# One DMA transpose for the keys of four heads in batches 2 and 3, in a talking-heads attention with a gated MLP behind it

## The chip, the core and the metric

The kernel runs on one core of one Trainium2 chip. The metric is the device time in microseconds, from the start of the program to its end on that core. Engines are named as in the profile: PE (matrix multiplications), DVE (vector), ACT (scalar), POOL (GpSimd), SP (the engine that issues all DMAs but three small ones at the start).

## The reference

Four batches, 12 heads, 448 positions, 64 numbers per head. The heads are mixed before and after the softmax, and the result goes through a gated MLP.

```
scores = (q @ k^T) / 8                            # per batch and head: 448 x 448
scores = einsum('bhij,hg->bgij', scores, w_pre)   # mix of heads
attn   = softmax(scores)
attn   = einsum('bhij,hg->bgij', attn, w_post)    # mix of heads
x      = attn @ v                                 # 448 x 768 per batch
u, v_  = split(gelu(x @ w_in))                    # 512 and 512 columns
gated  = u * (w_sg @ layernorm(v_) + b_sg)        # w_sg is 448 x 448
out    = x + gated @ w_out
```

## The kernel before, in words

Work goes by chunks of up to 128 query rows, four per batch, 16 in all; here they are called chunk 0 to chunk 15, so batch 1 is chunks 4 to 7, batch 2 is 8 to 11 and batch 3 is 12 to 15. A number is carried as a high and a low part in 16 bits, and a product of two such numbers is three matmuls.

`qk` (lines 961 to 1003) multiplies queries and keys of two heads (of four in the first, short chunk of a batch); the scores are scaled and copied out of PSUM, written to DRAM (`s_d`, line 958) and read back in groups of ten query rows over all heads (`g`, lines 1031 and 1037). Then come the first mix of heads (`ps_s`), the softmax (DVE maximum, ACT exponential, DVE reciprocal, a small scaling `wp` that is mostly on POOL), the second mix (`at`), the product with v (`ps_av`), and the MLP (`ps_v`, `ps_u`, `ps_x`). The MLP of one batch is done while the scores of the next are made: it is PE's filler around the change of batch.

Both operands of `qk` need the 64 numbers of a head along the partitions, so keys and queries are transposed. For batches 0 and 1 TensorE transposes the keys. For batches 2 and 3 (`B_DT = 2`) it is done by DMA, in `load_k`, in three loads per batch of four heads each (called K0, K1 and K2 here, for heads 0 to 3, 4 to 7 and 8 to 11). One load runs through these steps: SP fetches the 32-bit keys from DRAM (lines 548 and 550, three DMAs; for batches above 0 the last 64 positions are fetched twice, into partitions 0 to 63 and 64 to 127); two casts and two subtractions (lines 442 and 445, in the trace all on POOL) write the high and low parts into a staging tile of 16 bits, tag `sp`; SP transposes from the staging tile into `kT`. The queries of chunks 8 to 15 take the same way (`load_q`, line 489: one DMA transpose of twelve blocks of 128x128), through the same staging tile. **There is one buffer with the tag `sp`.** So K0, K1, K2 and the queries of each chunk use it one after the other: the next cast waits until the transposes before it have landed.

A load's transposes must also wait until the chunk of the batch before has used the keys that they overwrite: K0 of batch 2 waits for the `qk` of chunk 7 over heads 0 to 3, and so on.

The order of all instructions is fixed when the program is built, by a planner (`Plan`, line 252): it keeps a clock per engine, and picks among the streams of work by rank, plus a small random number (`jit`, seeded by `SEED`). A step on SP has a cost for the DMA engines and a number of issues (370 ns each on SP's clock): `(2500, 5)` for a load's transposes. Each engine then executes its instructions strictly in that order, and a semaphore holds an engine until what it needs is there. When the real times differ from the planned ones, an engine stands at an instruction that is not ready, with ready ones queued behind it.

Of the kernel before, what the change touches and what calls it, by code (L numbers as in the profile page):

```python
# [11 lines left out]
F16 = mybir.dt.float16  # L12
# [31 lines left out]
N_P32 = 3  # L44
N_PRE = 8
C_PRE = 800
SEED = 42
JIT = 0.2
SPIN = 110
SPIN_GAP = 200  # L50
# [57 lines left out]
def talking_heads_gmlp(ctx, tc, q, k, v, w_pre, w_post, w_in, g_ln, w_sg, b_sg, w_out, out):  # L108
    nc = tc.nc
    B, H, S, D = q.shape  # L110
# [3 lines left out]
    P = 128  # L114
# [3 lines left out]
    NC = S // TC  # L118
    JF = S // P
    JL = S - JF * P  # L120
    NA = JF * H + H // 2
    CQ = 120
    NCH = (S + CQ - 1) // CQ
# [13 lines left out]
    HG = 4  # L137
# [6 lines left out]
    ORD = (0, 1, 2, 3)  # L144
# [13 lines left out]
    const = ctx.enter_context(tc.tile_pool(name="const", bufs=1))  # L158
# [55 lines left out]
    mskc_t = vn_hi.rearrange("p c f -> p (c f)")[:, 504:520].bitcast(F32)  # L214


    kT = const.tile([P, H // HG, 2, HG // 2, S], F16, name="kT")
    qT2 = [const.tile([P, 2, H // 2, P], F16, name=f"qT{i}") for i in range(2)]
    v32 = const.tile([P, NA, D], F32, name="v32")
    at32 = const.tile([P, NA, AW], F32, name="at32")  # L220
# [39 lines left out]
    class Plan:  # L260
# [8 lines left out]
        def __init__(self):  # L269
# [7 lines left out]
            self.size = {}  # L277
            self.rnd = random.Random(SEED)

# [6 lines left out]
        def free(self, *names):  # L286
            return self.after([self.res.get(n, 0) for n in names])

        def seen(self, *names):
            return self.after([self.tm.get(n) for n in names])  # L290
# [4 lines left out]
        @staticmethod  # L295
        def after(times):
            return None if None in times else max(times)
# [6 lines left out]
        def give(self, t, *names):  # L304
            for n in names:
                assert self.res[n] is None, n
                self.res[n] = t
# [95 lines left out]
    def ones(n):  # L403

        return {"act": 100 + 0.9 * n, "dve": Shared(70 + 0.52 * n), "pool": 75 + 1.06 * n}
# [28 lines left out]
    free, seen, past, after, take, give, chain = pl.free, pl.seen, pl.past, pl.after, pl.take, pl.give, pl.chain  # L434


    def cast(o, i, scale=1.0, e=None):
        e = e or pl.on
        if e is nc.scalar:
            e.activation(out=o, in_=i, func=AF.Copy, scale=scale)  # L440
        else:
            e.tensor_scalar(out=o, in0=i, scalar1=scale, scalar2=1.0, op0=ALU.mult, op1=ALU.mult)  # L442

    def diff(o, a, b, e=None):
        (e or pl.on).tensor_tensor(out=o, in0=a, in1=b, op=ALU.subtract)  # L445
# [8 lines left out]
    def turn(ps, src, width):  # L454

        for n, x in enumerate(src):
            rows = x.shape[0]
            tr(ps[:, n * width:n * width + rows], x, ident32[:rows, :rows])
# [6 lines left out]

    def turn_k(hg, t, a, ps):
        turn(ps, [t[:, a, cc] for cc in range(JF)] + [t[:JL, a, JF]], P)
        return (ps[:, :S], *(kT[:, hg, k, a, :] for k in range(2)))

    def load_q(i):  # L470
        rank = K_Q12[i - 1] if i < 3 else fin[i - 1] - K_Q
# [49 lines left out]
    def load_kv():  # L521
        todo = [(b * GPB + (0, 3, 6)[hg] + (3 if b else 0), "v", b, hg) for b in range(B) for hg in range(H // HG)]
        for b in range(1, B):
            i = NCH * b - 1
            for hg in range(H // HG):
                todo.append((fin[i] + hg * HG * (fin[i + 1] - fin[i]) // H - K_KV, "k", b, hg))
        todo.sort()
        for rank, kind, b, hg in todo:
            if kind == "v":
                if ("v", b, hg) not in tm:  # L530
                    t = yield "sp", 2000, rank, 0, lambda: seen(("av", b - 1, ORD[-1])) if b else 0
                    fetch_v(b, hg, t)
                continue
            t = yield "sp", 2000, rank, 0, lambda: free(ring("st"), ring("sp"))
            load_k(b, hg, rank + 1, t)

    def fetch_v(b, hg, t):
        hs = slice(hg * HG, (hg + 1) * HG)
        nc.sync.dma_start(out=v32[:, hg * HG * JF:(hg + 1) * HG * JF].rearrange("p (h c) d -> p h c d", c=JF),
                          in_=v[b, hs, :JF * P].rearrange("h (p c) d -> p h c d", c=JF))  # L540
        if hg == H // HG - 1:
            for f in range(2):
                nc.sync.dma_start(out=v32[f * JL:(f + 1) * JL, JF * H:], in_=v[b, f * H // 2:(f + 1) * H // 2, JF * P:].rearrange("h p d -> p h d"))
        tm["v", b, hg] = t

    def fetch_k(b, h0, x):
        hs = slice(h0, h0 + HG)
        nc.sync.dma_start(out=x[:, :, :JF], in_=k[b, hs, :JF * P].rearrange("h (p c) d -> p h c d", c=JF))
        for f in range(2 if b else 1):
            nc.sync.dma_start(out=x[f * JL:(f + 1) * JL, :, JF], in_=k[b, hs, JF * P:].rearrange("h p d -> p h d"))  # L550
# [9 lines left out]
    def load_k(b, hg, rank, t0):  # L560
        h0 = hg * HG
        x, xname = staged("st")
        y, name = staged("sp")
        k32 = y.rearrange("p t a c b d -> p (t a c b d)").bitcast(F32).rearrange("p (a c e) -> p a c e", a=2, c=NC)
        fetch_k(b, h0, x)

        def turns_by_dma(t):
            for part in range(2):
                t = yield None, (ones, twos)[part](HG * NC * D), rank, t
                for a in range(2):  # L570
                    o = y[:, part, :, :, a, :]
                    if part:
                        diff(o, x[:, a::2], y[:, 0, :, :, a, :])
                    else:
                        cast(o, x[:, a::2])
            give(t, xname)
            t = yield "sp", (2500, 5), rank, t, lambda: seen(("qk", NCH * b - 1, h0 + HG - 1))
            for w in range(2):
                for a in range(HG // 2):
                    nc.sync.dma_start_transpose(out=kT[:, hg, w, a, :JF * P].rearrange("p (c j) -> p c j", c=JF),  # L580
                                                in_=y[:, w, a, :JF].rearrange("p c b d -> p (c b d)"))
                    nc.sync.dma_start_transpose(out=kT[:, hg, w, a, JF * P:], in_=y[:JL, w, a, JF].rearrange("p b d -> p (b d)"))  # L582
            give(t, name)
            tm["k", b, hg] = t

        def turns(t):
            t = yield None, ones(HG * NC * D), rank, t
            for a in range(2):
                side(pl.on, k32, x, a)
            give(t, xname)  # L590
            ends = []
            for a in range(2):
                t1 = yield "pe", 4 * C_TR, rank, t, lambda: after([work_free(), seen(("qk", NCH * b - 1, h0 + HG - 1))])
                ps, bank_name = work_bank("ps_k")
                split(rank, t1, turn_k(hg, k32, a, ps), S, bank_name, ends)
            give(t1, name)
            yield None, {"pool": 0}, rank, t1, lambda: max(ends) if len(ends) == 2 else None
            tm["k", b, hg] = max(ends)

        pl.add((turns_by_dma if b >= B_DT else turns)(t0))  # L600
# [6 lines left out]
    def ring(kind):  # L607
        return f"{kind}{stn[kind] % {'st': 2, 'sp': 1}[kind]}"

    def staged(kind):  # L610

        name = ring(kind)
        stn[kind] += 1
        take(name)
        if kind == "st":
            return st32.tile([P, HG, NC, D], F32, tag="st", name="st32"), name
        return st16.tile([P, 2, HG // 2, NC, 2, D], F16, tag="sp", name="st16"), name
# [196 lines left out]
    def work_free():  # L814
        return free(f"wk{works[0] % 2}")
# [47 lines left out]
    def part_mm(s, hg, ps):  # L863
        for n, (tq, tk) in enumerate(((0, 0), (0, 1), (1, 0))):
            for o in range(2):
                for a in range(2):
                    r = slice(a * D, (a + 1) * D)
                    m = QP * (2 * o + a)
                    mm(ps[m:m + QP, :S], lhsT=qT2[0][r, tq, 2 * hg + o, PART[s]:PART[s] + QP],
                                     rhs=kT[r, hg, tk, o, :], start=(n == 0), stop=(n == 2))  # L870

    def part_hi(s, hg, ps, eng=None):
        cast(e0[s][:, hg, 0], ps[:, :S], 1.0 / math.sqrt(D), eng)
# [45 lines left out]
    def qk_mm(i, h, pss):  # L919

        rows = q_rows(i)
        for n, (tq, tk) in enumerate(((0, 0), (0, 1), (1, 0))):
            for o in range(heads(i) // 2):
                w = 64 if quarters(i) else rows
                for c in range(0, rows, w):
                    m = min(w, rows - c)
                    for a, ps in enumerate(pss):
                        r = slice(a * D, (a + 1) * D)
                        mm(ps[o * rows + c:o * rows + c + m, :S], lhsT=qT2[i % 2][r, tq, h // 2 + o, c:c + m],
                                         rhs=kT[r, h // HG, tk, h // 2 % 2 + o, :], start=(n == 0), stop=(n == 2))  # L930

    def qk_place(i, h):
        if (i, h) in early:
# [106 lines left out]
    st = {}  # L1040
# [556 lines left out]
    with tc.manual_schedule():  # L1597
# [13 lines left out]
        for i, w in enumerate((w_pre, w_post)):  # L1611
# [4 lines left out]
                              in_=ident32[:H, :H].unsqueeze(1).unsqueeze(1).to_broadcast([H, 2, NH, H]))  # L1616
# [201 lines left out]
```

## Time and profile before

| | |
|---|---|
| median of three runs | 612.03 us (611.52 to 621.69) |
| the profiled execution | 613.37 us, of which the traced span is 611.6 us |
| PE busy | 573.4 us (94%) |
| ACT, DVE, POOL busy | 372.0, 362.2, 221.7 us (61%, 59%, 36%) |
| PE's share of the chain that ended last | 79%; DMA 6%, SP's queue 4% |
| instructions in the trace | 25,636 |

The chain that ended last is followed back from the last instruction to what released each step; where it is on PE, PE had work and did it, and where it is on a DMA or on SP's queue, PE was waiting for that. A window is a stretch of the span, in us from its start; the granted clock (PEclk) is 1.00 at 2.4 GHz and 0.50 at 1.2 GHz, and between them where a stretch has both.

### The profile page before, as it was taken

To read this page: it belongs to the slowest core of one execution; us is meant where nothing else is said; L and a number is where in the kernel's file an instruction comes from. 1 tells how busy PE (TensorE), PEld (TensorE's weight loads), DVE (VectorE), ACT (ScalarE), POOL (GpSimd) and SP (SyncE) were. 2 spreads that over 40 slices of the span, in tenths; PEclk is the share of its full clock that TensorE was granted. 3 is DMA by queue.
4 is the path that set the end of the run, shared out by engine and by line. 5 is a ranking of instruction groups with operands and counts; after the bars stand their busy time and mean duration, and the time that the engine had idled before them with its cause. 6 is when DMAs were issued, how large, how long until landed. Compare 5 with 4: busy or idle time off the path is not lost.

```text
span 611.6 us, 25636 instructions
## 1 busy us (share of the span) xinstructions
PE 573.4 (94%) x10847; PEld 382.3 (62%) x10847; DVE 362.2 (59%) x945; ACT 372.0 (61%) x911; POOL 221.7 (36%) x392
## 2 busy tenths in 40 slices
PE   8997999999999979489999989789999999999997
PEld 4555766577665637257766756446765857678654
DVE  6865487666667533246777655336768764355560
ACT  5776697786867535346877555446766665655231
POOL 6424255774455363223413463123312252121100
PEclk9998999999999999889999997879999999999999
DMA  9887999986888396399898775399796745420002
GB/s 201 240 250 219 246 303 263 212 246 201 243 270 252 101 223 162 84 226 267 203 250 244 171 203 165 93 247 248 145 273 181 202 125 171 121 73 4 1 2 91
DMA packets 110611, 113.48 MB, mean 186 GB/s; under 512 B 60852, under 2 KB 97724, under 8 KB 110496
## 3 DMA queue, kind: packets, MB, share of 16 engines
q1 hardware_dynamic: 110432, 111.84, 68.2%
q8 instruction: 85, 1.39, 1.0%
q14 instruction: 30, 0.25, 0.2%
q10 hardware_dynamic: 64, 0.00, 0.0%
HBM read 64.20 MB, written 42.10 MB: 174 GB/s over the span
## 4 chain that ended last, share of the span: by engine, by line
PE 79%; DMA 6%; SPq 4%; issue 3%; POOL 2%; ACT 2%; DVE 2%; POOLq 0%; ACTq 0%; DVEq 0%
PE at L236 15%; PE ps_s L236 12%; PE ps_x L236 12%; PE ps_av L236 10%; PE ps_v L236 9%; PE ps_qk L236 9%; PE ps_u L236 9%; DMA qT<-st 2%; DMA g<-s_d 1%; DMA s_d<-s 1%; SPq L580 1%; SPq L582 1%; PE ps_q L240 1%; POOL st L445 1%; DMA v<-in_v_dram 1%
## 5 line engine op out<-in xcount | busy, mean ns | idle before, releaser
L1077 DVE TENSOR_REDUCE nm<-ps_s 128x1 f32<-128x448 f32 x180 | 105.6, 618 | 47.6 <-PE ps_s L236 46.4
L1084 ACT ACTIVATE p<-ps_s,nm 128x448 f32<-128x448 f32 x180 | 113.7, 632 | 30.1 <-DVE nm L1077 29.5
L236 PEld LDWEIGHTS at<-wp,p 64*64 64x64 f32 x5364 | 108.8, 139 | 32.2 <-issue 19.8
L440 ACT ACTIVATE at<-at 128x420 f32<-128x420 f32 x179 | 99.2, 567 | 45.6 <-PE at L236 44.8
L236 PE MATMUL at<-wp,p 64*64 64x60 f32 (+1 forms) x5364 | 114.8, 223 | 6.8 <-issue 4.1
L442 POOL TENSOR_SCALAR wp<-wpc,rs 128x60 f32<-128x60 f32 x139 | 46.5, 336 | 193.5 <-DVE rs L1090 146.8
L440 ACT ACTIVATE s<-ps_qk 128x448 f16<-128x448 f32 (+3 forms) x134 | 68.4, 546 | 35.6 <-PE ps_qk L236 26.5
L236 PE MATMUL ps_qk<-kT,qT 64*64 64x448 f16 (+3 forms) x1080 | 72.8, 360 | 16.5 <-DMA qT<-st 11.2
L236 PE MATMUL ps_av<-at,v 128*64 128x120 f32 (+3 forms) x1536 | 71.2, 261 | 1.4 <-issue 1.4
L236 PEld LDWEIGHTS ps_av<-at,v 128*64 128x64 f32 (+1 forms) x1536 | 65.0, 135 | 9.5 <-issue 6.5
L949 DVE SCALAR_TENSOR_TENSOR s<-ps_qk,s 128x448 f16<-128x448 f32 x84 | 49.8, 618 | 26.5 <-ACT s L440 25.7
L236 PE MATMUL ps_u<-xTh,wbuf 128*128 128x256 f16 (+1 forms) x384 | 61.3, 260 | 0.0
L236 PE MATMUL ps_x<-wo,gbuf 128*128 128x384 f16 (+1 forms) x336 | 58.5, 339 | 0.0
L1089 DVE TENSOR_SCALAR rs<-ss 128x1 f32<-128x1 f32 x180 | 26.9, 149 | 52.3 <-ACT p L1084 50.5
L236 PEld LDWEIGHTS <-wbuf 128*128 128x128 f16 x576 | 50.2, 98 | 11.1 <-issue 6.6
L236 PEld LDWEIGHTS <-qT 64*64 64x64 f16 (+3 forms) x1080 | 30.1, 106 | 42.8 <-issue 13.2
L236 PE MATMUL ps_s<-g,wpre 60*64 60x448 f32 x324 | 46.9, 571 | 4.1 <-ACT p L1084 4.0
L236 PE MATMUL ps_u<-xTl,wbuf 128*128 128x192 f16 (+1 forms) x192 | 49.8, 259 | 0.0
L236 PEld LDWEIGHTS <-gbuf 128*128 128x128 f16 (+1 forms) x384 | 31.0, 103 | 23.5 <-issue 8.0
L1313 DVE SCALAR_TENSOR_TENSOR xTl<-ps_av,xTh 128x360 f16<-128x360 f32 (+1 forms) x32 | 15.3, 501 | 41.8 <-ACT xTh L440 41.8
L236 PEld LDWEIGHTS <-xTh 128*128 128x128 f16 (+1 forms) x336 | 24.5, 102 | 22.5 <-issue 11.3
L440 ACT ACTIVATE xTh<-ps_av 128x360 f16<-128x360 f32 (+1 forms) x31 | 12.4, 450 | 41.3 <-PE ps_av L236 41.3
(215 smaller groups left out, 903.1 us busy)
## 6 DMA issues: line engine op xcount, KB each, us to landing
g<-s_d SPq DMA_DIRECT2D x166, 210.0 KB
s_d<-s SPq DMA_DIRECT2D x18, 448.0 KB
s_d<-s SPq DMA_DIRECT2D x24, 280.0 KB
v<-in_v_dram SPq DMA_DIRECT2D x12, 384.0 KB
out_dram<-ot SPq DMA_DIRECT2D x24, 192.0 KB
s_d<-s SPq DMA_DIRECT2D x18, 252.0 KB
s_d<-s SPq DMA_DIRECT2D x18, 224.0 KB
s_d<-s SPq DMA_DIRECT2D x18, 196.0 KB
```

The source lines that it names most:

```text
L236: nc.tensor.matmul(ps, lhsT=lhsT, rhs=rhs, **kw)
L240: nc.tensor.transpose(*args)
L440: e.activation(out=o, in_=i, func=AF.Copy, scale=scale)
L442: e.tensor_scalar(out=o, in0=i, scalar1=scale, scalar2=1.0, op0=ALU.mult, op1=ALU.mult)
L445: (e or pl.on).tensor_tensor(out=o, in0=a, in1=b, op=ALU.subtract)
L580: nc.sync.dma_start_transpose(out=kT[:, hg, w, a, :JF * P].rearrange("p (c j) -> p c j", c=JF), in_=y[:, w, a, :JF].rearrange("p c b d -> ...
L582: nc.sync.dma_start_transpose(out=kT[:, hg, w, a, JF * P:], in_=y[:JL, w, a, JF].rearrange("p b d -> p (b d)"))
L949: nc.vector.scalar_tensor_tensor(out=e[:, 1, :], in0=ps[:n, :S], scalar=1.0 / math.sqrt(D), in1=e[:, 0, :], op0=ALU.mult, op1=ALU.subtract)
L1077: nc.vector.tensor_reduce(out=nm, in_=st[n]["s2"][:, :S], axis=AX.X, op=ALU.max, negate=True)
L1084: nc.scalar.activation(out=x["p32"], in_=x["s2"][:, :S], func=AF.Exp, bias=x["nm"], accum_out=x["ss"])
L1089: nc.vector.tensor_scalar(out=x["rs"], in0=x["ss"], scalar1=1e-9, scalar2=1.0 / S_P, op0=ALU.add, op1=ALU.mult)
L1313: nc.vector.scalar_tensor_tensor(out=dl, in0=src, scalar=isc, in1=dh, op0=ALU.mult, op1=ALU.subtract)
```

## The change

The eight DMA transposes of a load (for each part and each pair of heads one of three blocks of 128x128, and one that takes 64 partitions to 64 columns) become one of sixteen blocks of 128x128. To make that possible a row of `kT` gets 512 columns in place of 448: the last block is transposed whole, with the second copy of the 64 positions in columns 448 to 511, which nobody reads. The places that read `kT` take the first 448 columns. The planner's figures change with it: `(2800, 5)` for the transposes, `(2200, 3)` for the fetch of keys, `(2400, 3)` for the last fetch of v, and another seed.

```diff
-SEED = 42
+SEED = 21
...
-    kT = const.tile([P, H // HG, 2, HG // 2, S], F16, name="kT")
+    kT = const.tile([P, H // HG, 2, HG // 2, NC * P], F16, name="kT")
...
-        return (ps[:, :S], *(kT[:, hg, k, a, :] for k in range(2)))
+        return (ps[:, :S], *(kT[:, hg, k, a, :S] for k in range(2)))
...
-                    t = yield "sp", 2000, rank, 0, lambda: seen(("av", b - 1, ORD[-1])) if b else 0
+                    t = yield "sp", (2400, 3) if hg == H // HG - 1 else 2000, rank, 0, lambda: seen(("av", b - 1, ORD[-1])) if b else 0
...
-            t = yield "sp", 2000, rank, 0, lambda: free(ring("st"), ring("sp"))
+            t = yield "sp", (2200, 3), rank, 0, lambda: free(ring("st"), ring("sp"))
...
-            t = yield "sp", (2500, 5), rank, t, lambda: seen(("qk", NCH * b - 1, h0 + HG - 1))
-            for w in range(2):
-                for a in range(HG // 2):
-                    nc.sync.dma_start_transpose(out=kT[:, hg, w, a, :JF * P].rearrange("p (c j) -> p c j", c=JF),
-                                                in_=y[:, w, a, :JF].rearrange("p c b d -> p (c b d)"))
-                    nc.sync.dma_start_transpose(out=kT[:, hg, w, a, JF * P:], in_=y[:JL, w, a, JF].rearrange("p b d -> p (b d)"))
+            t = yield "sp", (2800, 5), rank, t, lambda: seen(("qk", NCH * b - 1, h0 + HG - 1))
+            nc.sync.dma_start_transpose(out=kT[:, hg].rearrange("p t a (c j) -> p (t a c) j", c=NC),
+                                        in_=y.rearrange("p t a c b d -> p (t a c b d)"))
...
-                                     rhs=kT[r, hg, tk, o, :], start=(n == 0), stop=(n == 2))
+                                     rhs=kT[r, hg, tk, o, :S], start=(n == 0), stop=(n == 2))
...
-                                         rhs=kT[r, h // HG, tk, h // 2 % 2 + o, :], start=(n == 0), stop=(n == 2))
+                                         rhs=kT[r, h // HG, tk, h // 2 % 2 + o, :S], start=(n == 0), stop=(n == 2))
```

Since the planner's figures and its seed change, the order of the whole program changes, on every engine. The amount of work does not: PE has the same matmuls but for two used to pass the time, and only a few copies go to another engine. Three places around the change of batch matter below.

SP, from the fetch of K2 of batch 2 to the transpose of the first queries of that batch (chunk 8, into `qT_124`), before. `st_4346` holds fetched keys, `st_4347` is the staging tile, `st_4642` the same buffer with queries:

```order
L548 DMA st_4346<-in_k_dram 128x4x192
L550 DMA st_4346<-in_k_dram 64x4x64 x2
L1563 DMA out_dram<-ot 64x384 x2
L1037 DMA g_120<-s_d_136 60x2x448 x2
L1563 DMA out_dram<-ot 128x384
L580 DMA_TRANSPOSE kT<-st_4347 128x3x128
L582 DMA_TRANSPOSE kT<-st_4347 128x64
...
L1563 DMA out_dram<-ot 128x384
L1037 DMA g_119<-s_d_136 60x2x448 x2
L489 DMA_TRANSPOSE qT_124<-st_4642 128x12x64
```

The same queue of the changed kernel, from the transpose of K0 of batch 2 to the fetch of K1 (`st_4134`); the writes to `s_d_136` are scores of chunk 7:

```order
L578 DMA_TRANSPOSE kT<-st_3689 128x16x128
L955 DMA s_d_136<-s_3857 128x896
L955 DMA s_d_136<-s_3893 128x896
L1034 DMA g_119<-s_d_136 60x2x448 x2
L1034 DMA g_120<-s_d_136 60x2x448 x2
L489 DMA_TRANSPOSE qT_124<-st_4005 128x12x64
L955 DMA s_d_136<-s_4064 128x896
L452 DMA q_91<-in_q_dram 56x12x64
L452 DMA q_91<-in_q_dram 72x12x64
L548 DMA st_4134<-in_k_dram 128x4x192
L550 DMA st_4134<-in_k_dram 64x4x64 x2
```

The queries of chunk 8 came after K2; now they come after K0, ahead of K1 and K2. Those of chunk 9 now stand between K1 and K2.

POOL, from the cast of K2 of batch 2 to the queries of chunk 8, before:

```order
L442 TENSOR_SCALAR st_4347<-st_4346 128x8x64 x2
L442 TENSOR_SCALAR wp<-wpc_101,rs 128x60
L445 TENSOR_TENSOR st_4347<-st_4346,st_4347 128x8x64 x2
L442 TENSOR_SCALAR wp<-wpc_101,rs 128x60 x2
L442 TENSOR_SCALAR st_4642<-q_91 64x768
L445 TENSOR_TENSOR st_4642<-q_91,st_4642 64x768
L442 TENSOR_SCALAR wp<-wpc_101,rs 128x60 x4
```

POOL in the changed kernel, from the cast of K0 of batch 2 (`st_3689`) through the queries of chunk 8 (`st_4005`); `vs` and `gbuf` are the gate of batch 1's MLP:

```order
L442 TENSOR_SCALAR st_3689<-st_3688 128x8x64 x2
L442 TENSOR_SCALAR wp<-wpc_101,rs 128x60
L445 TENSOR_TENSOR st_3689<-st_3688,st_3689 128x8x64 x2
L442 TENSOR_SCALAR wp<-wpc_101,rs 128x60 x3
L442 TENSOR_SCALAR st_4005<-q_91 64x768
L1504 TENSOR_TENSOR vs<-vs,gbuf 128x448
L445 TENSOR_TENSOR st_4005<-q_91,st_4005 64x768
L1504 TENSOR_TENSOR vs<-vs,gbuf 128x448
L445 TENSOR_TENSOR gbuf<-vs,gbuf 128x448 x2
```

The cast of queries now stands behind K0 and ahead of most of the gate, where it was behind K2 and behind the whole gate.

PE, just ahead of the first `qk` of chunk 8 (it reads `qT_124`), before; the last `qk` of chunk 7 is 295 rows further up, and between the two stand 128 matmuls of `ps_x`, 24 of `ps_s`, 192 of `at` and 48 of `ps_av`:

```order
L236 MATMUL ps_x<-wo,gbuf 128x384
L236 LDWEIGHTS xTh_129
L236 MATMUL ps_x<-ident_x,xTh_129 128x128
L236 LDWEIGHTS xTl_130
L236 MATMUL ps_x<-ident_x,xTl_130 128x128
...
L236 LDWEIGHTS qT_124
L236 MATMUL ps_qk<-kT,qT_124 64x448
```

The same place in the changed kernel, from the last matmul of chunk 7's `qk` (it reads `qT_125`):

```order
L236 MATMUL ps_qk<-kT,qT_125 64x448
L236 MATMUL ps_s_4302<-g_119,wpre_98 64x448 x2
L236 MATMUL ps_s_4303<-g_119,wpre_98 64x448 x2
L236 MATMUL at_472<-wp,p_112 64x60 x12
L236 MATMUL at_472<-wp,p_108 64x60 x12
L236 MATMUL at_472<-wp,p_112 64x30 x4
L236 MATMUL at_472<-wp,p_108 64x30 x4
L236 LDWEIGHTS qT_124
L236 MATMUL ps_qk<-kT,qT_124 64x448
```

The first `qk` of chunk 8 has moved ahead of most of batch 1's MLP: it stands directly behind chunk 7, and the rest of that MLP now lies between the `qk` of chunk 8 that need K0, K1 and K2: 30 matmuls of `ps_x` ahead of the one for K1, 90 more ahead of the one for K2.

## Rows read from the trace of the kernel before

**Rows 1.** The page's first part: busy us, share of the span, instructions.
```profile
PE 573.4 (94%) x10847; PEld 382.3 (62%) x10847; DVE 362.2 (59%) x945; ACT 372.0 (61%) x911; POOL 221.7 (36%) x392
```

**Rows 2.** Windows by stage: stretch, its length, busy us of each engine, PEclk, DMA share, GB/s.
```profile
197.00:276.00 79.00, 65.21 (x1304) 40.79 (x1301) 31.79 (x91) 36.47 (x93) 28.28 (x45) 0.91 0.66 159
276.00:340.00 64.00, 63.43 (x1402) 44.48 (x1398) 47.54 (x130) 47.38 (x119) 24.63 (x45) 1.00 0.92 242
340.00:410.00 70.00, 59.89 (x1175) 39.21 (x1177) 33.40 (x87) 33.11 (x83) 24.56 (x35) 0.88 0.65 168
```

**Rows 3.** Waits of PE from 197 to 276 us: us in total, times, longest.
```profile
PE ps_qk L236 <- DMA qT<-st: 9.7, 1, 9.7
PE ps_s L236 <- ACT p L1084: 4.0, 2, 2.7
```

**Rows 4.** Waits of PE from 340 to 410 us.
```profile
PE ps_qk L236 <- DMA kT<-st: 4.9, 3, 2.2
PE ps_s L236 <- ACT p L1084: 3.1, 2, 2.6
PE ps_qk L236 <- DMA qT<-st: 1.5, 1, 1.5
```

**Rows 5.** Timeline of SP's queue, K2 of batch 2: start, us, what.
```profile
233.24 0.41 SPq L548 DMA_DIRECT2D st<-in_k_dram  x1
...
241.72 1.23 SPq L580 DMA_TRANSPOSE kT<-st  x1
```

**Rows 6.** Timeline of POOL there, with its idle time before and what ended it.
```profile
240.49 1.20 POOL L442 TENSOR_SCALAR st<-st 128x512 f16<-128x512 f32 x2 [4.19 <-DMA g<-s_d]
...
241.94 2.28 POOL L445 TENSOR_TENSOR st<-st,st 128x512 f16<-128x512 f32 x2
...
255.58 0.82 POOL L442 TENSOR_SCALAR st<-q 64x768 f16<-64x768 f32 x1 [10.77 <-DMA g<-s_d]
```

**Rows 7.** The chain that ended last, 195 to 262 us: start, us, what.
```profile
196.88 0.91 PE ps_s L236 x8
197.79 4.62 PE ps_av L236 x96
...
204.22 1.06 PE at L236 x64
205.28 0.57 PE ps_qk L236 x12
...
252.88 2.39 DMA kT<-st
...
258.14 3.31 DMA qT<-st
```

**Rows 8.** The same chain, 340 to 412 us.
```profile
348.27 2.94 PE ps_x L236 x15
...
385.93 2.39 PE ps_x L236 x18
...
400.98 6.72 DMA qT<-st
```

**Rows 9.** Instructions of kT and of qT: ns shortest/median/longest, first and last start.
```profile
L582 SPq DMA_TRANSPOSE kT<-st x24: 1202/1227/2506, 200.9 to 395.7; - x24
...
L489 SPq DMA_TRANSPOSE qT<-st x8: 1252/1654/3193, 258.1 to 439.3; - x8
```

**Rows 10.** Windows in which PE's clock was low while it worked, columns as above.
```profile
227.00:232.00 5.00, 5.00 (x85) 2.89 (x82) 1.89 (x6) 1.96 (x6) 1.27 (x3) 0.66 0.23 46
262.00:266.00 4.00, 4.00 (x87) 2.29 (x83) 1.69 (x3) 1.48 (x4) 1.78 (x2) 0.67 0.97 265
...
368.30:374.00 5.70, 5.70 (x98) 3.94 (x97) 3.03 (x11) 2.99 (x8) 1.83 (x3) 0.51 0.22 43
...
398.10:406.00 7.90, 7.51 (x100) 4.44 (x100) 2.63 (x6) 2.86 (x7) 3.39 (x6) 0.59 1.04 255
```

**Rows 11.** The window over K2's transposes, columns as above.
```profile
242.00:252.00 10.00, 9.78 (x192) 6.04 (x190) 4.54 (x17) 7.25 (x20) 2.81 (x4) 1.00 0.19 39
```

## The prediction

> **What bounds the kernel now.** I read the page first. PE is busy 573.4 of 611.6 us and no other engine passes 61% [rows 1], so the kernel is PE's work plus the time in which PE stands or runs slowly, and the second part is all that this change can touch: 38.2 us stand idle. Then I cut the span by stage to see where. The two stretches around a change of batch, 197 to 276 and 340 to 410 us, have PE busy 65.2 of 79.0 and 59.9 of 70.0 us [rows 2]: 13.8 and 10.1 us idle, 23.9 of the 38.2. The stretch between them loses 0.6 of 64. So outside the two changes of batch PE loses 14.3 us in 462.6, some 3%.
>
> The idle time costs more than itself. The granted clock in these stretches is 0.91 and 0.88 on the mean [rows 2], and after each wait PE works at 1.2 GHz for some microseconds [rows 10]. Work lost is length times one minus the clock: 5.0 x 0.34 = 1.7, 4.0 x 0.33 = 1.3, 5.7 x 0.49 = 2.8, 7.9 x 0.41 = 3.2, together 9.0 us. So the two changes of batch cost 23.9 + 9.0 = 32.9 us above PE's work at full clock.
>
> The waits of PE say for what. At the first change it is one wait of 9.7 us for the queries' transpose, and 4.0 us for ACT's exponential [rows 3]; at the second 4.9 us for the keys' transposes, 1.5 us for the queries' and 3.1 us for the exponential [rows 4]. What stands behind the 9.7 us is told by SP, POOL and the chain of waits: K2's fetch is issued at 233.24, POOL casts from 240.49 and subtracts to 244.2, SP issues eight transposes from 241.72 [rows 5, 6], the last at 252.88, and that lands 2.39 us later, at 255.27 [rows 7]; only then is the staging tile free, POOL casts chunk 8's queries at 255.58 (it stood 10.77 us, with four `wp` queued behind) [rows 6], and their transpose goes out at 258.14 and lands after 3.31 us [rows 7]. PE starts again at 261.5. So one tile, held from cast to landing, is what is late, and 13.6 us of each hold (241.72 to 255.27) are transposes.
>
> **What the change removes.** An issue of one block of 64 columns takes 1.2 us of SP [rows 9], one of three blocks 1.23 [rows 5], one of twelve 1.25 to 3.19, median 1.65 [rows 9]. So an issue is priced by the piece, hardly by its blocks: eight take at least 9.6 us, one takes 1.3 to 3.2. That issues and not the transfer fill the 13.6 us shows in the DMA share, 0.19 while K2's transposes run [rows 11].
>
> The new transpose is not in the trace. The nearest rows are the queries' of twelve blocks, issue to landing 3.31 and 6.72 us [rows 7, 8], the second with the DMA engines full (share 1.04) [rows 10]. Scaled by 16/12: 4.4 and 9.0 us. Since waits that vanish bring the traffic closer to that of 276 to 340 us (share 0.92) [rows 2], I take 8, nearer the loaded row, and 6 for the queries'. Each load's transposes then shrink from 13.6 to 8, by 5.6 us (4.6 to 9.2 at the ends). One loss goes against it: before, the first transposes went out while POOL still subtracted (241.72 against 244.2) [rows 5, 6]; one transpose of the whole tile must wait for both, 2.5 us. So the net is 3.1 us for each load, 2.1 to 6.7 at the ends, three loads at each change of batch. The 14% more blocks (16 for 14) are in the 8; the longer rows of `kT` cost PE nothing, since it reads 448 columns as before.
>
> The Trainium skill (Advanced Engine Details and Errata, X-Bar Transpose (TRN2)) says that transpose DMAs on TRN2 run as fast as others, 350 to 400 GB/s. An estimate from that page: sixteen blocks of 32 KB, 524 KB, in 1.5 us at 350. The trace doesn't bear it out: twelve blocks, 393 KB, in 3.31 us are 119 GB/s [rows 7]. By the page's rate the new waits in the sum below would go, and it would come to 585.
>
> **What the new order asks for.** I count from t, the end of chunk 7's (then chunk 11's) `qk` over heads 2 and 3, for which K0's transpose waits. Prices of PE's work are from the chain: 64 `at` records (32 in the order) 1.06, 96 `ps_av` (48 in the order) 4.62, 8 `ps_s` (4 in the order) 0.91, 12 `qk` 0.57 [rows 7], `ps_x` and the like 0.13 each, and 0.20 in the gate [rows 8].
>
> First change. From t to chunk 8's first `qk` PE has 160 `at` (5.3), 16 `ps_s` (3.6), 72 `ps_x` (48 of the gate, some of them half-height pairs; 11), 9 `ps_u` (1.2) and four `qk` (2.3): t+23. To the `qk` that needs K1 it is 12 more, t+36; to that for K2 some 20 more, t+56. The loads: K0's transpose goes out at t+2, behind a score write, and lands at t+10. POOL casts and subtracts chunk 8's queries, with a product of the gate between, in 5.5 us; their transpose goes out at t+15.5 and lands at t+21.5, before PE asks. K1's fetch stands two issues behind it, t+17.5; fetch to cast takes 7.3 us (233.24 to 240.49), cast and subtraction 3.7 [rows 5, 6]: out at t+28.5, landed at t+36.5, 0.5 late. Then chunk 9's queries take the tile (2.5 us), K2's fetch follows their transpose at t+41, cast from t+48.5, out at t+52, landed at t+60: 3.5 late.
>
> Second change. Chunk 12's queries were transposed long before. PE has some 38 us from t to the `qk` for K0 and 44 to that for K2. K2's fetch is held on SP by the scores of heads 8 and 9, to t+25.5: cast t+33, out t+36.5, landed t+44.5, 0.5 late.
>
> So 4.5 us of new waits remain, at the half clock seen after each [rows 10] some 6. Before, PE did batch 1's whole MLP by 251.8 and then stood; now it is spread between the three loads. The exponential's waits (4.0 and 3.1) hang on POOL: `wp` stood behind casts that waited for late keys [rows 6]. They go with the lateness; a cast that waits for one landing remains, in front of the gate.
>
> **The sum**, against the profiled execution, 613.4 us (1.3 above the median of three, 612.0): minus 32.9 for the two changes of batch, plus 3% of their 149 us, 4.6, as everywhere else, plus 6 of new waits: 591.1. I say **591**.
>
> At nothing I cost the new order elsewhere. It is covered by the engines' slack alone (POOL 36%, DVE 59%, ACT 61% busy) [rows 1]; a new draw can win or lose part of the 14.3 us that PE stands idle outside the two stretches, say 5 either way. SP's time saved (some 8 us per load, of a queue that also issues scores and `g`) I cost at nothing too: it only moves transfers earlier.
>
> **Rivals.**
> - *The loaded end and POOL's new place.* At 9 us per transpose and 6.7 for the queries' the same count gives 8.7 us of waits, some 11 with the clock: 596. What could add to it is POOL: the cast of chunk 8's queries now stands in front of nine products of the gate. If K0's transpose is held up on SP by a score write, the gate slips by as much, and with it the output products meant to fill PE: 8 to 10 us back, 600 to 606. For it: full stretches have a DMA share of 0.92 to 1.04 [rows 2, 10], and POOL did stand 10.77 us at such a cast [rows 6]. Against: the means at the changes of batch are 0.66 and 0.65 [rows 2].
> - *The transfer is what takes the time* (slower). If the 13.6 us were transfer and not issue, sixteen blocks would take 15.5. In the new order, with chunk 9's queries between K1 and K2 and no overlap with the subtraction, the count gives: chunk 8's first `qk` 3 us late, K1 12, K2 11, and K2 of the second change 12: 38 us where 23.9 stood, at like clock about 627. It decides from some 12 us per transpose, where the waits equal the old ones. Against it stand the share of 0.19 [rows 11] and twelve blocks in 3.31 to 6.72 [rows 7, 8]. The Trainium skill (DMA: Bandwidth & Descriptors, Issuing engines are not separate DMA queues) speaks for it: the sequencer's time to start a DMA is usually small relative to the DMA itself. By that rule fewer issues save next to nothing; here the trace contradicts it, with 9.6 us of issues in 13.6.
> - *The new draw loses elsewhere* what it wins here: 10 us more on PE's 14.3 give 601, 20 give 611.
>
> **How the numbers follow.** The forecast, 580 to 599, gets 0.66; POOL's place 0.13; the new draw 0.14, nearly all of it within 2%; the transfer 0.07. Two per cent, about what a measurement of this kernel can tell from no change, is 599.8 and 624.3. Faster 0.66, within 0.26, slower 0.08 (the transfer, and 0.01 of the draw). The lower end is the sum without new waits, 585, and 5 us won by the draw: 580. The upper end takes in POOL's place and most of the draw: 611. Outside remain the transfer and a little on each side.
>
> **What would show it.** In the profile of the changed kernel: six issues at line 578, of 1.3 to 3.2 us, in place of 48; each lands in 4.4 to 9 us (15 or more: the transfer). PE's wait of 9.7 us for `qT<-st` gone, waits for `kT<-st` below 5 us each; idle time in the two changes of batch together at most 12 us, and the granted clock there above 0.95. POOL's waits in front of the queries' casts 5 to 7 us in place of 10.77. If these hold and the time is above 600, the draw took it, and the stretch that lost it shows in the windows. The forecast is wrong if a transpose takes over 10 us, or if PE finds a new wait at the moved `qk`.

## The result, and the profile after

The changed kernel takes 578.06 us (median of four, 576.36 to 580.17), the kernel before 616.86 (median of four, 611.52 to 627.43). The ratio is 0.9451, with a 95% interval from 0.9389 to 0.9512; it leaves out the executions of a slower state, here two of the kernel before (621.69 and 627.43), and so goes by its other two, 611.52 and 612.03. The change is faster, by more than was forecast: 591 stood in the prediction, and 578 lies just below its lower end, 580. The profiled execution took 576.36 us, 37.0 less than the one of before (613.37).

The page of the changed kernel: its span, the engines' busy time (as [rows 1] of before), the granted clock in 40 slices, and the chain that ended last.

```profile
span 574.6 us, 25573 instructions
...
PE 560.2 (97%) x10845; PEld 377.2 (66%) x10845; DVE 362.6 (63%) x942; ACT 376.5 (66%) x925; POOL 218.0 (38%) x381
...
PEclk9999999999999998999999999999999999999999
...
PE 89%; DMA 4%; ACT 2%; issue 2%; DVE 2%; POOL 1%; SPq 0%; ACTq 0%; POOLq 0%
```

PE does the same work in 560.2 us in place of 573.4, and stands idle for 14.4 in place of 38.2. So 23.8 of the 37.0 us are idle time, and 13.2 are busy time, most of it work that was done at a low clock before (see the sizes below).

The changed kernel's windows around the two changes of batch and between them, as [rows 2] show them of before (length, busy us of each engine, PEclk, DMA share, GB/s):

```profile
190.00:262.00 72.00, 68.74 (x1412) 42.90 (x1406) 37.29 (x102) 43.08 (x110) 32.54 (x46) 0.98 0.96 215
262.00:325.00 63.00, 62.80 (x1399) 45.12 (x1391) 46.66 (x125) 46.48 (x116) 22.58 (x41) 1.00 0.91 233
325.00:385.00 60.00, 58.08 (x1298) 38.49 (x1296) 36.84 (x97) 37.87 (x96) 26.25 (x40) 1.00 0.94 231
```

PE is idle for 3.3 and 1.9 us where it was idle for 13.8 and 10.1, the clock is 0.98 and 1.00 for 0.91 and 0.88, and the DMA engines, idle for a third of the time before, are as full there as between. What PE still waits for, at the first change (190 to 265 us) and then at the second (325 to 385), against [rows 3, 4]:

```profile
PE at L236 <- issue: 2.8, 2, 1.9
PE ps_s L236 <- issue: 0.3, 1, 0.3
```
```profile
PE ps_qk L236 <- DMA qT<-st: 1.2, 1, 1.2
PE at L236 <- ACT at L440: 0.7, 1, 0.7
```

The 9.7 us for the queries, the waits for keys and those for the exponential are gone. The transposes themselves, as [rows 9] (ns shortest, median, longest; first and last start), and two on the chain of waits, from issue to landing: the last of the keys', and the queries' of chunk 13 behind it:

```profile
L578 SPq DMA_TRANSPOSE kT<-st x6: 2867/3188/3910, 196.7 to 356.9; - x6
...
L489 SPq DMA_TRANSPOSE qT<-st x8: 1232/1741/2245, 207.1 to 402.6; - x8
```
```profile
356.92 7.22 DMA kT<-st
...
367.94 6.86 DMA qT<-st
```

### The profile page after: what moved, and what is told of

Its sections match the earlier page's. It is cut to its first block, busy times and chain, and to the rows that moved or that the text cites. A ratio compares the mean times of both kernels' runs of the same rounds, so it can differ in the third digit from the quotient of the medians.

```text
span 574.6 us, 25573 instructions
## 1 busy us (share of the span) xinstructions
PE 560.2 (97%) x10845; PEld 377.2 (66%) x10845; DVE 362.6 (63%) x942; ACT 376.5 (66%) x925; POOL 218.0 (38%) x381
## 4 chain that ended last, share of the span: by engine, by line
PE 89%; DMA 4%; ACT 2%; issue 2%; DVE 2%; POOL 1%; SPq 0%; ACTq 0%; POOLq 0%
PE at L236 17%; PE ps_x L236 15%; PE ps_s L236 13%; PE ps_av L236 12%; PE ps_u L236 10%; PE ps_v L236 10%; PE ps_qk L236 8%; DMA kT<-st 1%; DMA qT<-st 1%; DMA xTh<-in_moe_w_in_dram 1%; PE ps_warm L236 1%; PE ps_spin L236 1%; ACT s L440 1%; DMA s_d<-s 1%; PE ps_q L240 0%
## 5 line engine op out<-in xcount | busy, mean ns | idle before, releaser
L236 PEld LDWEIGHTS at<-wp,p 64*64 64x64 f32 x5364 | 104.2, 136 | 29.0 <-issue 16.4
L442 POOL TENSOR_SCALAR wp<-wpc,rs 128x60 f32<-128x60 f32 x133 | 43.6, 328 | 198.3 <-DVE rs L1087 159.0
L236 PE MATMUL at<-wp,p 64*64 64x60 f32 (+1 forms) x5364 | 110.5, 219 | 4.7 <-issue 2.8
L236 PE MATMUL ps_qk<-kT,qT 64*64 64x448 f16 (+3 forms) x1080 | 68.9, 354 | 1.5 <-DMA qT<-st 1.2
L236 PEld LDWEIGHTS <-wbuf 128*128 128x128 f16 x576 | 50.1, 98 | 11.7 <-issue 7.1
L236 PE MATMUL ps_x<-wo,gbuf 128*128 128x384 f16 (+1 forms) x336 | 56.2, 331 | 0.0
L236 PE MATMUL ps_s<-g,wpre 60*64 60x448 f32 x324 | 44.0, 551 | 1.1 <-issue 1.1
L236 PEld LDWEIGHTS <-qT 64*64 64x64 f16 (+3 forms) x1080 | 27.7, 104 | 25.7 <-issue 11.9
L1081 ACT ACTIVATION_READ_ACCUMULATOR p<-ps_s,nm 128x1 f32 x180 | 37.5, 208 | 0.0
L440 ACT ACTIVATE xTh<-ps_av 128x360 f16<-128x360 f32 (+1 forms) x31 | 12.4, 449 | 35.4 <-PE ps_av L236 35.4
```

Source lines behind the costliest of these rows:

```text
L236: nc.tensor.matmul(ps, lhsT=lhsT, rhs=rhs, **kw)
L1081: nc.scalar.activation(out=x["p32"], in_=x["s2"][:, :S], func=AF.Exp, bias=x["nm"], accum_out=x["ss"])
```

## The experiments

Two theories stood against each other at first. By the prediction, **the staging tile** is what is late: one buffer, held from cast to landing. By the other, **SP's queue** is: eight issues stand in front of the next fetch and of the queries' transpose, whichever buffer they use. A third question was what the new order, the other half of the change, is worth.

**1. The one transpose alone, in the order of before.** The longer rows and the new transpose, with the planner's costs and seed of before; so every engine but SP has its instructions as before.

```diff
 t = yield "sp", (2500, 5), rank, t, ...
-for w in range(2):
-    for a in range(HG // 2):
-        (two transposes)
+nc.sync.dma_start_transpose(out=kT[:, hg].rearrange("p t a (c j) -> p (t a c) j", c=NC),
+                            in_=y.rearrange("p t a c b d -> p (t a c b d)"))
```

> The kernel before with the one transpose and the longer rows alone: planner's figures and seed as before, so every engine has the order of before, row by row, but for the transposes. Theory A (the hold of the staging tile is what costs): each load's hold shrinks from 13.6 us to some 8, the 9.7 us wait for the queries and most of the 9.5 us of the second change go, with the low clock behind them: 583 to 592 us. Theory B (the new order is what pays, with chunk 8's queries moved ahead of K1 and the MLP spread between the loads): little comes of the transpose alone, 600 to 610. Theory C (the seed's draw): 605 or more.

579.41 us, ratio 0.9378 (0.9312 to 0.9444): the gain of the whole change, and somewhat more than theory A expected (583 to 592). Its windows at the two changes of batch:

```profile
197.00:260.00 63.00, 62.75 (x1329) 40.60 (x1330) 33.79 (x94) 38.93 (x100) 28.73 (x45) 1.00 0.88 212
330.00:390.00 60.00, 59.26 (x1389) 39.90 (x1388) 40.57 (x107) 39.59 (x102) 26.45 (x39) 1.00 0.93 228
```

PE idles there for 0.3 and 0.7 us. This kernel is the cleanest measure, because its order is that of before. SP's timeline in it (start, us, what), and then the first issues for K0 and K1 in the kernel before (K2's first and the queries' are in [rows 5, 7]):

```profile
200.26 3.21 SPq L578 DMA_TRANSPOSE kT<-st  x1
...
217.20 3.33 SPq L578 DMA_TRANSPOSE kT<-st  x1
...
234.06 1.77 SPq L578 DMA_TRANSPOSE kT<-st  x1
...
241.18 1.23 SPq L489 DMA_TRANSPOSE qT<-st  x1
```
```profile
199.55 1.31 SPq L580 DMA_TRANSPOSE kT<-st  x1
...
220.17 1.26 SPq L580 DMA_TRANSPOSE kT<-st  x1
```

| step | before | one transpose | gained |
|---|---|---|---|
| K0's to K1's | 199.55 to 220.17: 20.6 | 200.26 to 217.20: 16.9 | 3.7 |
| K1's to K2's | 220.17 to 241.72: 21.6 | 217.20 to 234.06: 16.9 | 4.7 |
| K2's to the queries' | 241.72 to 258.14: 16.4 | 234.06 to 241.18: 7.1 | 9.3 |

The queries go out 17.7 us earlier counted from K0's, more than the 13.8 us for which PE had stood.

**2. The new order alone**: the changed kernel with the eight transposes in place of the one.

> The changed kernel with the eight transposes of before in place of the one: the new order alone. A: the count of the prediction with holds of 13.6 us in the new order gives some 34 us of waits at the changes of batch where 23.9 stood, so 610 to 630. B: the order carries most of the gain, 590 or less. C: like B.

613.87 us, ratio 0.9946 (0.9907 to 0.9985). So the order by itself is worth half a per cent, at most one; it waits for the same late keys, in other places:

```profile
PE ps_qk L236 <- DMA kT<-st: 8.9, 5, 2.2
PE ps_s L236 <- ACT p L1084: 6.5, 3, 4.0
PE ps_qk L236 <- DVE s L949: 4.5, 1, 4.5
```

**3 and 4. What a draw is worth.** The changed kernel with `SEED = 1` for 21, and the kernel before with `SEED = 21` for 42.

> The changed kernel with the seed 1. A: 575 to 590, as the hold is as short in every order. C: the seed 21 is a lucky draw, 595 or more.

> The kernel before with the seed 21 alone. A and B: the same lateness in another draw, 605 to 622. C: the draw is what pays, 580 to 595.

585.3 us, ratio 0.9483 (0.9425 to 0.9541), and 618.43 us, ratio 1.0097 (1.0036 to 1.0158). A draw moves either kernel by about 1%, and neither seed explains the gain.

**5. Two staging tiles**, in the order of before, SP's included: `bufs=1` becomes `bufs=2` for the tag `sp`. This is the test of the prediction's own story.

> The kernel before with two buffers for the staging tile in place of one; the planner knows nothing of it, so every engine's order is that of before, the eight transposes too. Theory A1 (the staging tile is what is late, as the prediction put it): a cast no longer waits for the landing of the transposes before it, the waits at the changes of batch shrink to the length of a landing: 585 to 597 us. Theory A2 (SP's queue is what is late: the next fetch of keys and the queries' transpose stand behind ten microseconds of issues): only the landings of 2.4 us and the early cast of chunk 8's queries are won, 602 to 611.

615.91 us, ratio 0.9953 (0.9896 to 1.001): no gain that can be told, and above both ranges, A2's too. POOL's row of the cast of chunk 8's queries, and SP's rows of K2's first and last transpose and of the queries', with two tiles:

```profile
247.60 0.83 POOL L442 TENSOR_SCALAR st<-q 64x768 f16<-64x768 f32 x1
```
```profile
244.44 1.23 SPq L580 DMA_TRANSPOSE kT<-st  x1
...
254.70 1.23 SPq L582 DMA_TRANSPOSE kT<-st  x1
...
258.46 1.25 SPq L489 DMA_TRANSPOSE qT<-st  x1
```

The cast no longer waits for the tile, it starts 8 us earlier than before (255.58 [rows 6]). But its transpose stands behind K2's eight on SP and goes out at 258.46, where it went out at 258.14 before. PE waits as it did:

```profile
PE ps_qk L236 <- DMA qT<-st: 8.8, 1, 8.8
```

**6. One transpose, and SP held behind it.** Kernel 1 with seven more transposes of one block behind each load's, from a constant into a tile that nothing reads. The keys land early; only what stands on SP behind them is late.

```diff
+for n in range(7):
+    nc.sync.dma_start_transpose(out=idle_t[:, n], in_=ident)
```

> The one transpose in the order of before, and behind each of them seven transposes of one block of the identity into a tile that nobody reads: the staging tile comes free as early as with the one transpose, but SP issues for as long as before (seven times 1.2 us more). A1: 578 to 590. A2: most of the gain is lost, 600 to 615.

632.71 us, ratio 1.0272 (1.0197 to 1.0346): the whole gain goes, and more than A2 expected. SP's rows of K0 and K1, POOL's row of the cast of K1, PE's waits, and the chain that ended last at K2 and the queries behind it (L582 are the unread transposes, shown are the first and the last of seven):

```profile
202.47 3.27 SPq L579 DMA_TRANSPOSE kT<-st  x1
205.80 10.49 SPq L582 DMA_TRANSPOSE idle_t<-ident  x7
219.05 0.46 SPq L549 DMA_DIRECT2D st<-in_k_dram  x1
...
227.92 4.14 SPq L579 DMA_TRANSPOSE kT<-st  x1
```
```profile
224.44 1.21 POOL L443 TENSOR_SCALAR st<-st 128x512 f16<-128x512 f32 x2 [9.16 <-DMA st<-in_k_dram]
```
```profile
PE ps_qk L237 <- DMA qT<-st: 14.5, 2, 13.4
PE ps_s L237 <- DMA g<-s_d: 9.4, 4, 7.3
PE ps_s L237 <- ACT p L1084: 7.6, 4, 2.6
```
```profile
257.02 1.70 SPq L582
...
265.48 1.23 SPq L582
...
269.25 5.12 DMA qT<-st
```

Seven small issues hold SP for 10.5 us, K1's fetch goes out only behind them, and K0's to K1's transpose becomes 25.5 us where kernel 1 had 16.9. The cast of K1 waits 9.16 us, and for the fetch. It is the issue of the fetch that is late and not its transfer: from fetch to cast it takes 5.4 us here (219.05 to 224.44), and 7.1 in kernel 1 (206.31 to 213.39). That it is slower than before fits with two things: SP is held somewhat longer (13.0 us per load on the mean, 11.8 before), and before, the first transposes went out while POOL still subtracted, 2.5 us before its end [rows 5, 6], and here all of them stand behind the subtraction. The scores' way back (`g`), issued on SP too, is late as well: PE waits 9.4 us for it, where the kernel before shows 0.2. So what SP's hold costs is not the keys and queries alone.

**7 and 8. Half of that.** Kernel 1 with the same transpose issued twice, the second into a tile that nothing reads; and kernel 1 with four transposes of four blocks, `kT[:, hg, w, a]` each, for the one of sixteen.

> The one transpose in the order of before, and behind each a second one of the same sixteen blocks into a tile that nobody reads: the hold of the staging tile and SP's time grow by the price of one more. Both A1 and A2: some 3 to 4 us more per load on SP and on the tile, three loads on the path at each change of batch where the waits have just gone: 585 to 598 us. If transposes were hidden anyway: 579 to 582.

> The longer rows and four transposes of four blocks each in place of the one, in the order of before. If an issue is priced by the piece at 1.2 us: 4.9 us of issues and a landing of 2.4, as long as the one transpose in all: 578 to 586. If the price goes by blocks (the one transpose took SP 1.8 to 4.4 us): likewise some 5 us, the same range. If one transpose is what matters (one landing, one semaphore): 590 to 600.

595.38 us, ratio 0.9693 (0.9618 to 0.9768), and 589.63, ratio 0.9598 (0.9538 to 0.9657). The issues of the one and of the other:

```profile
L579 SPq DMA_TRANSPOSE kT<-st x6: 2882/3090/4272, 200.2 to 370.2; - x6
...
L581 SPq DMA_TRANSPOSE idle_t<-st x6: 2077/3016/3967, 203.4 to 374.3; - x6
```
```profile
L580 SPq DMA_TRANSPOSE kT<-st x24: 1213/1274/2388, 200.7 to 372.8; - x24
```

Four blocks cost SP as much as one, 1.27 us. I had expected 578 to 586 of the four pieces, and that missed: they hold SP for some 6 us per load, as the two of kernel 7 do. With kernels 1 and 6 and the kernel before this makes a row, all in the order of before. SP's time runs from the start of a load's first transpose to the end of its last, over the six loads of the profiled execution:

| kernel | SP on transposes, us per load: least to most, mean | time, us |
|---|---|---|
| 1: one | 1.8 to 4.4, 3.3 | 579.4 |
| 8: four of four blocks | 5.8 to 7.3, 6.5 | 589.6 |
| 7: one, twice | 5.0 to 8.3, 6.3 | 595.4 |
| before: eight | 11.0 to 12.4, 11.8 | 616 to 617 |
| 6: one and seven small | 11.7 to 13.8, 13.0 | 632.7 |

Counted from kernel 1 by the means, each microsecond of SP per load costs 3 to 5.5 us of time, with six loads in the kernel. Kernel 7 also doubles the transfers and holds the tile for longer (POOL's casts wait for it twice, 17.2 us in all; in kernel 1 they wait once, 7.8 us), which may be why it lies above kernel 8; that was not taken apart.

**9 and 11. Is the planner to blame?** It counted 5 issues (1.85 us) where eight take 11.0 to 12.4. The kernel before with 28 issues, `(2500, 28)`, and the changed kernel with 9, `(2800, 9)`, near what SP really takes.

> The kernel before, with its eight transposes, but the planner is told how long SP takes to issue them: 28 issues of 370 ns, 10.4 us, in place of 5. Theory Q (SP's time is on the path, whatever the order; by the four doses so far one us of SP per load costs 5 us in all): 605 to 618. Theory P (the planner's blindness is what costs: it plans fetches and casts too early, and an order that knows of the ten microseconds hides them): 580 to 598.

> The changed kernel with the planner told what the one transpose takes of SP: nine issues, 3.3 us, in place of five. Q: the order is drawn anew, within the spread of the draws seen so far (1%), 572 to 586. P: a truer plan is a better one, below 572.

627.0 us, ratio 1.0164 (1.0097 to 1.0232), and 580.15, ratio 0.9414 (0.9331 to 0.9497). Told the truth the planner finds nothing better, and with eight issues something worse than either theory expected. Whether some other order would hide them is not shown: one draw of each was run.

**10. The transposes on ACT's queue**: kernel 1 with `nc.scalar` for `nc.sync` at keys and queries, so that SP is free of them altogether.

> The one transpose, and the queries' transposes too, issued by ACT in place of SP, in the order of before. Q: SP is freed of another 3.2 us per load and 1.5 us per chunk of queries, but ACT, 65% busy, stands for as long and waits in order for POOL's subtraction and for the tile: the exponentials behind it are late. If SP's time alone counts: 560 to 572. If ACT's place in the softmax chain counts as much: 585 to 610.

599.8 us, ratio 0.9758 (0.9683 to 0.9833), 20 above kernel 1. Issues (ACT's queue), two rows of ACT with the idle time before them, one landing on the chain that ended last, and two waits of PE:

```profile
L578 ACTq DMA_TRANSPOSE kT<-st x6: 2765/3879/4590, 201.8 to 373.8; - x6
```
```profile
206.38 0.34 ACT L440 ACTIVATE wp<-wpc,rs 128x60 f32<-128x60 f32 x1 [3.87 <-issue]
...
392.08 0.56 ACT L440 ACTIVATE at<-at 128x420 f32<-128x420 f32 x1 [8.57 <-issue]
```
```profile
373.81 13.89 DMA kT<-st
```
```profile
PE at L236 <- issue: 5.4, 5, 3.0
PE ps_s L236 <- ACT p L1081: 4.5, 5, 2.1
```

The issue held ACT as it holds SP: the 3.87 us stand behind a transpose of keys issued at 201.80, for 4.53 us. The 8.57 us are another thing. There ACT stood in order at the transpose of queries until POOL had cast and subtracted them, and that cast had waited 13.77 us for the tile, because the last keys, issued at 373.81, landed only after 13.89 us. ACT stands in the softmax, between PE's two mixes. No kernel beats the changed one.

## Why the prediction was right, and where it was wrong

**What it had right.** PE bounds the kernel, and what can be won lies at the two changes of batch: 23.9 us idle and 9.0 us of work at low clock. Kernel 1 gives that back: 15.2 us idle for 38.2 (-23.0) and 564.4 us busy for 573.4 (-9.0). The transposes are priced by the piece far more than by their bytes (eight hold SP for 11.0 to 12.4 us, one with 14% more blocks for 2.9 to 3.9), so the rival in which the transfer takes the time falls: sixteen blocks land in 7.2 us (8 was taken, 4.4 to 9 the bounds), where eight pieces took 13.6. The Trainium skill (DMA: Bandwidth & Descriptors, Issuing engines are not separate DMA queues) calls the time to start a DMA usually small relative to the DMA itself. For small transposes it is not small here: before, an issue of 1.23 us [rows 9] stands in 2.39 us from issue to landing [rows 7], and in kernel 6 seven of 32 KB hold SP for 10.5 us. Of the rival of a loaded end the traffic came (DMA shares of 0.96 and 0.94, 6.86 us for the queries of chunk 13), but not its waits; the draw that loses did not come about.

**The step that failed: what is late.** The prediction named the staging tile, and it costed SP's saved time at nothing ("it only moves transfers earlier"). Kernel 5 takes the tile's wait away and wins nothing that can be told; kernel 6 leaves the tile nearly as kernel 1 has it (from K2's transpose to the cast of queries 6.0 us for 4.6) and loses everything. What is late before is SP's queue. Its time was not beside the path: a load is fetch, cast, subtraction, transpose, and the next load's fetch stands on SP behind that transpose, and the queries' behind the last. In the profile of before it stood to be read: POOL's cast of K2 had waited 4.19 us before 240.49 [rows 6], with a fetch that SP issued only at 233.24 [rows 5]; the row names `g` as what ended that wait, in kernel 6 the same kind of wait is named as the fetch. So the chain's landing was taken for the cause, where the row of issues in front of it was. The forecast could come out near all the same, because the one transpose shortens both, the tile's hold and SP's.

The tile is not nothing once SP is free. In the changed kernel K2 of batch 3 lands at 364.14, POOL casts chunk 13's queries at 364.29, and these land at 374.80: PE waits 1.2 us for them. In kernel 10 the same hold lasts 13.89 us. Two staging tiles together with the one transpose were not run.

**The sizes.** The forecast was 22.3 us below the profiled execution and the change brought 37.0. By terms, in the changed kernel's trace:

| term | predicted | measured |
|---|---|---|
| idle at the two changes of batch | -23.9 + 4.6 + 4.5 = -14.8 | 23.9 to 5.2: -18.7 |
| idle elsewhere | 0, draw 5 either way | 14.3 to 9.2: -5.1 |
| PE's busy time (clock) | -9.0 + 1.5 = -7.5 | -13.2, of it -9.5 clock (an estimate, below) |
| sum | -22.3 | -37.0 |

*New waits.* They were counted as 4.5 us, 6 with the clock, and none came; PE's idle time at the first change is its own issue. The count itself, from t = 196.6 (the end of the `qk` after which K0's keys may be overwritten), was good to some 2 us: K2's transpose was put at t + 52 and went out at 246.74, t + 50.1; K1's at t + 28.5, and it went out at 222.86, t + 26.3. K0's was put behind a score write and was not held. SP's rows of the changed kernel:

```profile
196.71 3.19 SPq L578 DMA_TRANSPOSE kT<-st  x1
...
207.11 1.23 SPq L489 DMA_TRANSPOSE qT<-st  x1
211.26 1.73 SPq L548 DMA_DIRECT2D st<-in_k_dram  x1
...
222.86 3.19 SPq L578 DMA_TRANSPOSE kT<-st  x1
...
246.74 2.87 SPq L578 DMA_TRANSPOSE kT<-st  x1
```

PE asked somewhat later than counted: chunk 8's first `qk` starts at 221.19, t + 24.6 and not t + 23, and the one for K2 at 254.33, t + 57.7 and not t + 56. With a landing of 7.2 us, the one that is shown, K2 is there at t + 57.3. Two microseconds on either side turned 3.5 us of lateness into none. And the residual of 4.6 us is not due in these stretches: kernel 1 leaves 1.0 us idle there.

*The gain per load* was put at 3.1 us (2.1 to 6.7). In the order of before it is 3.7 and 4.7 between loads, and 9.3 at the last, where the queries' transpose had stood behind landing and issues both: 5.9 on the mean, far from the value taken and within the bounds only by a misreading.

*The misreading.* The landing of 3.31 us [rows 7], from which the lower bound of 4.4 came, is that of chunk 8's queries, and chunk 8 is the short one of its batch: its transpose is 128x12x64 in the order of SP, and its cast 64x768 [rows 6]. So these are twelve blocks of half height (chunk 12's too, where the text on the kernel before says 128x128 of all), 197 KB and not 393, an estimate of 59 GB/s and not 119. Scaled by bytes they give 8.8 us for sixteen whole blocks, and the upper end of the gain becomes 2.3 and not 6.7. The shortest issue "of twelve blocks", 1.25 us, is that row too. The value taken, 8, came from the other row, of whole blocks, and was near.

*The clock.* Four windows were counted, 9.0 us, and that size was about right. With the whole span cut into windows of 2 us, PE's busy time in each times one minus the clock gives, as an estimate, 11.1 us of work lost before (9.5 of it in the two stretches, 1.6 at 52 to 58 us), 3.4 in kernel 1 (all at 106 to 116 us) and 1.6 in the changed kernel. So the clock gives back 9.5 of the 13.2 us by which the changed kernel is less busy, and 7.7 of the 9.0 of kernel 1, which meets the counted 9.0 by chance; where the rest arises was not settled. The clock also differs between executions of one kernel: kernel 1 took 576.36 and 577.45 us at a mean of 1.00, and 581.38 and 582.06 at 0.993 and 0.988.

*The new order* was argued at length as a help. It is worth nothing that can be told: kernel 2 stands within 1% of before, and kernel 1 without it at 579.41 beside 578.06. What it wins elsewhere (5.1 us of idle time) it gives back at the changes of batch (5.2 us idle where kernel 1 has 1.0). Its term, "at nothing, 5 either way", was right.

**What the profile was to show**: six issues of 1.3 to 3.2 us (2.9 to 3.9); landing in 4.4 to 9 (7.2); the wait of 9.7 us gone, waits for keys below 5 (none); at most 12 us idle (5.2); a clock above 0.95 (0.98 and 1.00); POOL's wait in front of the queries' cast 5 to 7 us. Ahead of chunk 8's queries it is gone altogether: they are cast at 203.45 right behind other work. Ahead of chunk 13's it is 2.83 us.

```profile
203.45 0.82 POOL L442 TENSOR_SCALAR st<-q 64x768 f16<-64x768 f32 x1
```

**What stays open**: why four pieces cost 10 us against one, and the second transpose of kernel 7 16, for some 3 us more of SP per load each; what a second tile is worth beside the one transpose; and where, in the kernel with ACT's issues, each of the 20 us arises.

## What to carry to other kernels

Where one engine issues all DMAs in order, count its issue time as work on the path wherever a fetch, a cast and a transpose form a chain: what was late before was the instruction behind the issues, and neither the buffer nor the bytes; with the issues short, the buffer came next. Merge small transposes into one, and look twice before you move them to an engine that stands in another chain. Before naming a wait's cause, take away the buffer in one kernel and hold the queue in another: both cost a few lines, and here they gave opposite answers.

## What the runs showed of the hardware

An issue of one block of 128x128 holds SP for 1.23 us in the median (kernel 6), one of four blocks for 1.27 (kernel 8). In the changed kernel it is 1.2 to 1.3 for twelve blocks of half height, 1.5 to 2.3 for twelve whole ones and 2.9 to 3.9 for sixteen, where the prediction expected 1.3 to 3.2. The number of blocks is not all of it. The same sixteen took SP 1.8 to 4.4 us in kernel 1, and the shortest issue is the one during which the DMA engines had little else to do, with a share of 0.31; during the five others it is 1.00 and more. Two of these windows (columns as in [rows 2]):

```profile
200.26:203.50 3.24, 3.24 (x73) 3.08 (x72) 0.97 (x5) 1.58 (x5) 1.84 (x3) 1.00 1.07 193
234.06:235.83 1.77, 1.77 (x75) 1.35 (x68) 1.50 (x4) 0.93 (x3) 0.00 (x0) 1.00 0.31 64
```

On ACT's queue (kernel 10) the issue of sixteen takes 2.8 to 4.6 us.

From issue to landing sixteen blocks, 524 KB, take 7.22 us in the changed kernel, in a stretch where the DMA engines, with other traffic on them too, are 94% busy; that is an estimate of 73 GB/s for the one transpose. Kernel 11 shows one of 5.92 us, kernel 10 one of 13.89. The Trainium skill (Advanced Engine Details and Errata, X-Bar Transpose (TRN2)) expects 350 to 400 GB/s per core of transpose DMAs; no transpose measured here comes near that by itself.
